# Weight maxima of two experts: from reloaded halves, or from the units as they pass

## The chip, the core and the metric

The kernel runs on one core of one Trainium2 chip. The metric is the device time of one execution in microseconds (us); the time given for a kernel is the median of its runs. A core has five engines that each work through their own queue in order: TensorE (PE, matrix products), VectorE (DVE), ScalarE (ACT), GpSimd (POOL) and SyncE (SP), which here issues nearly all DMA transfers.

## The reference, cut to what matters

Four batches of eight heads of causal attention with a decay, 576 positions of 64 columns, give x with 2304 rows of 512 columns. A mixture of four experts follows, with weights by domain and no routing: every row goes through every expert.

```python
scores = scale * q @ k.T + (cum[:, None] - cum[None, :])      # causal
x = softmax(scores) @ v                                       # 2304 x 512
p = domain_probs / domain_probs.sum(-1)
for e in range(4):
    h = relu(x @ w1[e])                                       # 512 -> 1024
    out += p[:, e:e+1] * (h @ w2[e])                          # 1024 -> 512
```

## The kernel before

**Two forms of a product.** Every product of float32 numbers is made from parts. In the first sweep over the weights a weight unit is split into a rounded part wh and a rest wl, both 128x1024 in a 32-bit matmul format. In the second sweep, and in everything behind it, the parts are float16, and a unit must first be scaled by a power of two that fits the largest weight of its expert. That is why the maximum of each expert's weights is needed, for w1 and w2 apart.

**Units and steps.** The weights of an expert lie in eight units of 128x1024 (512 KB): 512 columns of w1 and 512 of w2. Units 0 to 31 are the first sweep's, 32 to 63 the second's, with unit n holding the same numbers as n - 32. A step takes two units over a chunk of 256 rows of x: l1 (x times w1), a gate (gh on ACT, gl on DVE) and, while the next step's l1 is under way or done, l2. Two steps make a group of four units, and acc on DVE adds up each group. The name l1_0_6_2_1 means sweep 0, group 6 (expert 3 has groups 6 and 7), chunk 2, second half of the group. The first sweep has 28 steps (chunk 0 for every expert, 1 for experts 2 and 3, 2 for expert 3), at 60 to 250 us or so; steps 28 to 79 are the second sweep. Attention for the later chunks runs between: s is a score, p its exponential, z and pt its float16 parts before and behind a transposing DMA, o the product with v, and x of a chunk is made of four head pairs (0 to 3). y is x in float16; topx and ux find the scale of a chunk.

**Where maxima came from.** `w_peek(e, i)` loads half a unit (128x512, 256 KB) into the tile pk with a DMA on SP and, two steps on, reduces it on DVE to a column of wmax. For expert e it is called in 16 steps beginning at PEEK[e]: 1, 15, 31 and 45. In step PEEK[e] + 17 (18, 32, 48, 62) `w_scale(e)` follows: its first part reduces wmax to wm on DVE, writes wm to DRAM (dw) and reads it back spread over all partitions into tops; the second part, three steps later, makes the scale wsc and its inverse wun. `w_split(n)` takes a loaded unit wr: in the first sweep ACT rounds it to wh and DVE or POOL subtract to wl; in the second, it is scaled and split in float16, with assertions that its expert's scale is known. It then starts three later loads of units.

**What sets the order.** The program is written once, as a list of steps with attention's work spread by cost; a scheduler then gives each engine its queue from a model of the engines. A function under `behind` is kept behind the gl of the step before. `at_step(n, f)` runs f behind the gl in step n. An instruction added on one engine so moves others, on all engines.

Of the kernel before, what the change touches and what calls it, by code (L numbers as in the profile page):

```python
# [13 lines left out]
ALU = mybir.AluOpType  # L14
AX = mybir.AxisListType
# [12 lines left out]
    ((1, 2, 3, 4), (1, 2, 3, 4), (2, 3, 4), (3, 4)),  # L28
)
WIDE = (0, 1, 2)  # L30
PEEK = (1, 15, 31, 45)
V_PEEK = 1
PT = ("pth", "ptl", "ptx")
TURN = ((1, 14), (2, 18), (3, 24), (4, 28))
# [44 lines left out]
def fused(ctx: ExitStack, tc: tile.TileContext, qk, v, f, probs, w, out):  # L79
    nc = tc.nc  # L80
# [35 lines left out]
    wmax = const.tile([128, 2, 8, E], F32, name="wmax")  # L116
# [73 lines left out]
    def at_step(n, f):  # L190
        later.setdefault(n, []).append(f)
# [47 lines left out]
    def behind(f):  # L239
        if prev is None:  # L240
            f()
            return
        with tc.issue_after(prev.last.ins):
            f()
# [32 lines left out]
    def w_peek(e, i):  # L277

        n, k = divmod(i, 2)
        t = pk_p.tile([128, 512], F32, tag="pk", name=f"pk{e}_{i}")  # L280
        nc.sync.dma_start(out=t, in_=w[8 * e + n, :, 512 * k : 512 * k + 512])
        at_step(
            step + 2,
            lambda: nc.vector.tensor_reduce(
                out=wmax[:, k, n, e : e + 1], in_=t, op=ALU.max, axis=AX.X, apply_absolute_value=True
            ),
        )
# [57 lines left out]
    def v_peek(i):  # L345

        t = xf_p.tile([128, 1024], F32, tag=f"xf{2 + i % 2}", name=f"vp{i}")
        flat = v.rearrange("b r p t h d -> (b r p t h d)").rearrange(
            "(n p f) -> n p f", n=NV, p=128
        )  # L350
        nc.sync.dma_start(out=t, in_=flat[i])

        def top():
            with tc.issue_after(prev.first.ins):
                nc.scalar.activation(
                    out=t,
                    in_=t,
                    func=AF.Abs,
                    scale=1 / 1024,
                    accum_out=vmax[:, i : i + 1],  # L360
                )

        at_step(step + 2, top)
# [570 lines left out]
    def w_load(n):  # L934
        if n < NS and n not in wraw:
            wraw[n] = wr_p.tile([128, 1024], F32, tag="wr", name=f"wr{n}")
            nc.sync.dma_start(out=wraw[n], in_=w[n % 32])
# [3 lines left out]
    def w_pair(name):  # L941
        t = w_p.tile([128, 2, 1024], F16, tag=("wh", "wl")[len(pairs) % 2], name=name)
        pairs.append(t)
        return t

    def w_split(n):
        w_load(n)
        r = wraw.pop(n)
        if n < 32:
            wh[n] = w_p.tile([128, 1024], F32R, tag="wh", name=f"wh{n}")  # L950
            wl[n] = w_p.tile([128, 1024], F32R, tag="wl", name=f"wl{n}")
            nc.scalar.activation(out=wh[n], in_=r, func=AF.Copy)  # L952
            eng = nc.vector if n in W_DVE else nc.gpsimd
            for a in (0, 512):
                z = a + 512
                eng.tensor_tensor(  # L956
                    out=wl[n][:, a:z],
                    in0=r[:, a:z],
                    in1=wh[n][:, a:z].bitcast(F32),
                    op=ALU.subtract,  # L960
                )
        else:
            e = n % 32 // 8
            assert ("w", e) in known
            t = w_pair(f"w{n}")
            wh[n], wl[n] = t[:, 0], t[:, 1]
            for k in range(2):
                c = slice(512 * k, 512 * k + 512)
                sc = wsc[:, e, k : k + 1]
                if k == 1:  # L970
                    nc.gpsimd.tensor_scalar(  # L971
                        out=r[:, c], in0=r[:, c], scalar1=sc, scalar2=None, op0=ALU.mult
                    )
                    nc.scalar.activation(out=wh[n][:, c], in_=r[:, c], func=AF.Copy)
                    nc.gpsimd.tensor_tensor(
                        out=wl[n][:, c], in0=r[:, c], in1=wh[n][:, c], op=ALU.subtract
                    )
                    continue
                nc.scalar.activation(out=wh[n][:, c], in_=r[:, c], func=AF.Copy, scale=sc)
                nc.vector.scalar_tensor_tensor(  # L980
                    out=wl[n][:, c],
                    in0=r[:, c],
                    scalar=sc,
                    in1=wh[n][:, c],
                    op0=ALU.mult,
                    op1=ALU.subtract,
                )
            at_step(step + 2, lambda: nc.sync.dma_start(out=wd[n - 32], in_=t))
        w_load(n + 1)
        w_load(n + 2)  # L990
        w_load(n + 3)
# [629 lines left out]
    for n in range(len(steps) + 1):  # L1621
        step = n
        cur = steps[n] if n < len(steps) else None
        for f_ in later.pop(n, ()):
            behind(f_)
        for e, first_ in enumerate(PEEK):
            if 0 <= n - first_ < 16:
                w_peek(e, n - first_)
            if n == first_ + 17:
                a_, b_ = w_scale(e)  # L1630
                behind(a_)
                at_step(n + 3, b_)
        if 0 <= n - V_PEEK < NV:
            v_peek(n - V_PEEK)
        if n == V_PEEK + NV + 1:
            a_, b_ = v_scale()
            behind(a_)
            at_step(n + 2, b_)
        if cur is not None:
            if cur.c not in used:  # L1640
                used.add(cur.c)
                upto(need[cur.c])
            for c, m in TURN:
                if n >= m and c not in yh and ("x", c) in known:
                    narrow(c)
            if cur.s == 1:
                assert cur.c in yh
                weigh(cur.g // 2, cur.c)
            for q in range(4):
                cur.l1(q)  # L1650
                pace(n + q / 8)
            cur.gate()
        else:
            upto(len(asteps))
            chunks.close()
            late.h = late.enter_context(tc.tile_pool(name="h", bufs=4, side="right"))
            for e in range(E):
                weigh(e, LAST[0])
            big = [Big(p) for p in range(16)]
            turns = in_turns(0)  # L1660
            for _ in range(3):
                next(turns)()
        if prev is not None:
            for q in range(4):
                prev.l2(q)
                pace(n + (q + 4) / 8)
                if cur is None:
                    for _ in range(2 if q == 3 else 1):
                        next(turns)()
            for w0, t in ends.items():  # L1670
                if t is prev:
                    if w0 + 7 < NS:
                        w_split(w0 + 6)
                        w_split(w0 + 7)
                    first_units(w0)
        prev = cur
# [90 lines left out]
```

## Time and profile before

| | |
|---|---|
| median of 3 runs | 939.88 us (939.54 to 941.59) |
| the profiled execution | 939.25 us |
| span, first to last instruction | 937.5 us |
| PE, DVE, ACT, POOL busy | 885.3, 709.3, 568.9, 525.1 us |
| mean granted clock of TensorE | 0.985 |
| moved by DMA | 159.45 MB |

The span is 1.75 us shorter than the execution. A busy engine of 25 in a stretch of 25 us has no gap; a clock below 1.00 means that part of the stretch ran at the lower of two levels. An idle time in the timeline stands with the instruction that ended it, and with the engine, or the DMA, that came last.

### The profile page before, as it was taken

Reading aid. Unit: us, or ns where it says so; the run is one execution under the profiler, and the core shown is the slowest. Engines: PE = TensorE matmul, PEld = TensorE weight load, DVE = VectorE, ACT = ScalarE, POOL = GpSimd, SP = SyncE. Lnnn points to the kernel's source line nnn. Section 1 sums busy time; section 2 is a strip of 40 time slices with the busy share of each in tenths; the row PEclk is TensorE's granted clock in tenths of the full one; section 3 lists DMA queues with packets and bytes.
Section 4 is the critical chain, followed back from the end, with each engine's and each line's share of the span. In section 5 each row is a group of like instructions: output and inputs, shape, how many; then the busy total and the mean of one; then the engine's idle time right before and its main releaser. Section 6 shows DMA issues by size and latency. Waiting matters only on the chain. (4 is left out here: it accounts for less than half of the span.)

```text
span 937.5 us, 16657 instructions
## 1 busy us (share of the span) xinstructions
PE 885.3 (94%) x5783; PEld 620.8 (66%) x5783; DVE 709.3 (76%) x1458; ACT 568.9 (61%) x1137; POOL 525.1 (56%) x528
## 2 busy tenths in 40 slices
PE   4899998999998889999999989999998999999998
PEld 3699988999765556666666656654455664666547
DVE  5768665786888988789878887576778757786487
ACT  5869755465676778668666777355665345653350
POOL 4657865478533754327641684265778627785060
PEclk9999999999998988999999999999999999999999
DMA  7458844538879698988999699524322424232003
GB/s 264 146 176 295 291 126 164 186 119 313 227 189 198 152 293 195 311 156 212 306 288 158 119 328 236 135 67 142 129 91 81 145 68 125 79 107 74 23 1 91
DMA packets 147508, 159.45 MB, mean 170 GB/s; under 512 B 86148, under 2 KB 107328, under 8 KB 147424
## 3 DMA queue, kind: packets, MB, share of 16 engines
q1 hardware_dynamic: 147424, 158.39, 60.2%
q8 instruction: 45, 0.74, 0.3%
q14 instruction: 39, 0.32, 0.2%
HBM read 117.30 MB, written 21.65 MB: 148 GB/s over the span
## 5 line engine op out<-in xcount | busy, mean ns | idle before, releaser
L1012 PE MATMUL l<-y,w 128*128 128x256 f16 x1248 | 155.7, 275 | 0.0
L1012 PEld LDWEIGHTS <-w 128*128 128x128 f16 x1248 | 118.3, 99 | 30.6 <-issue 6.5
L644 ACT ACTIVATE p<-p,nm 128x576 f32<-128x576 f32 (+3 forms) x160 | 95.6, 598 | 52.4 <-DVE nm L629 43.5
L1045 PE MATMUL l<-w,gh 128*128 128x512 f16 x408 | 122.6, 383 | 4.8 <-DVE acc L1072 4.8
L714 DVE SCALAR_TENSOR_TENSOR z<-p,rs,z 128x384 f16<-128x384 f32 (+3 forms) x128 | 85.7, 694 | 12.6 <-ACT z L713 11.1
L1072 DVE SCALAR_TENSOR_TENSOR acc<-y,scg,acc 128x256 f32<-128x256 f32 (+1 forms) x164 | 81.1, 515 | 14.9 <-PE y L1283 14.7
L615 PE MATMUL s<-hi 128*128 128x384 f32 (+1 forms) x192 | 76.9, 406 | 16.1 <-DVE hi L577 8.9
L563 POOL CAST q<-raw 64x320 fp32r<-64x320 f32 (+1 forms) x56 | 26.0, 465 | 117.9 <-PE s L615 71.3
L1283 PE MATMUL m<-rh,bs 128*128 128x512 f16 x256 | 86.4, 379 | 0.0
L629 DVE CUSTOM_DVE_ANT_0 p<-s,mask 128x288 f32<-128x288 f32 (+2 forms) x160 | 74.8, 475 | 12.9 <-PE s L615 11.8
L571 POOL TENSOR_TENSOR kl<-raw,hi 64x576 fp32r<-64x576 f32 (+1 forms) x56 | 66.4, 1186 | 28.6 <-ACT hi L562 28.2
L1045 PE MATMUL l<-w,gl 128*128 128x512 f16 x204 | 77.1, 383 | 5.0 <-DVE gl L1026 5.0
L1209 POOL TENSOR_TENSOR bs<-wt,bs 128x512 f16<-128x512 f32 x32 | 38.4, 1201 | 75.7 <-ACT bs L1208 75.4
L971 POOL TENSOR_SCALAR wr<-wr,wsc 128x512 f32<-128x512 f32 x32 | 53.9, 1687 | 35.1 <-DMA wr<-in_w 25.5
L956 POOL TENSOR_TENSOR wl<-wr,wh 128x512 fp32r<-128x512 f32 x48 | 64.4, 1370 | 15.9 <-ACT wh L952 11.6
L713 ACT ACTIVATE z<-p,rs 128x384 f16<-128x384 f32 (+3 forms) x128 | 69.5, 589 | 4.6 <-issue 1.2
L1026 DVE SCALAR_TENSOR_TENSOR gl<-l,gh 128x512 f16<-128x512 f32 (+1 forms) x80 | 54.7, 684 | 19.1 <-ACT gh L1025 18.6
L1012 PE MATMUL l<-xh,wh 128*128 128x256 f32 x224 | 65.0, 292 | 0.8 <-ACT xh L857 0.8
L615 PE MATMUL s<-kl,q 66*128 66x384 f32 (+1 forms) x192 | 63.7, 336 | 2.2 <-DMA kl<-nc 2.2
L1283 PE MATMUL m<-rh,bw 128*128 128x512 f16 x191 | 64.4, 379 | 1.4 <-ACT r L1329 1.4
L1012 PE MATMUL l<-xl,wh 128*128 128x256 f32 x224 | 65.2, 291 | 0.0
L1045 PEld LDWEIGHTS <-gh 128*128 128x128 f16 x408 | 37.0, 98 | 42.2 <-issue 11.2
(387 smaller groups left out, 2359.6 us busy)
## 6 DMA issues: line engine op xcount, KB each, us to landing
wr<-in_w SPq DMA_DIRECT2D x90, 512.0 KB
pk<-in_w SPq DMA_DIRECT2D x64, 256.0 KB
wd<-w SPq DMA_DIRECT2D x32, 512.0 KB
raw<-in_qk SPq DMA_DIRECT2D x32, 448.0 KB
bw<-wd SPq DMA_DIRECT2D x32, 256.0 KB
bv<-wd SPq DMA_DIRECT2D x32, 256.0 KB
raw<-in_qk SPq DMA_DIRECT2D x24, 256.0 KB
vp<-in_v SPq DMA_DIRECT2D x10, 512.0 KB
```

What stands on the lines that cost most here:

```text
L571: eng.tensor_tensor(out=kl[:64, :wk], in0=r[:64, ko : ko + wk], in1=hi[:64, ko : ko + wk].bitcast(F32), op=ALU.subtract,)
L615: nc.tensor.matmul(out=ps[:, at : at + z - a], lhsT=lhsT, rhs=rhs, start=(m == 0), stop=(m == 1),)
L629: nc.vector.tensor_tensor_reduce(out=pt[:, a:z], in0=ps, in1=mask[:, m0 + a : m0 + z], scale=-0.125, scalar=BIG if n == 0 else nm[:, col : ...
L644: nc.scalar.activation(out=pt[:, :w_], in_=pt[:, :w_], func=AF.Exp, scale=-1.0, bias=self.nmax[hh][:, c : c + 1], accum_out=self.ssum[:, h ...
L713: nc.scalar.activation(out=o[:, 0], in_=x, func=AF.Copy, scale=sc)
L714: nc.vector.scalar_tensor_tensor(out=o[:, 1], in0=x, scalar=sc, in1=o[:, 0], op0=ALU.mult, op1=ALU.subtract)
L956: eng.tensor_tensor(out=wl[n][:, a:z], in0=r[:, a:z], in1=wh[n][:, a:z].bitcast(F32), op=ALU.subtract,)
L1012: nc.tensor.matmul(out=self.l1p[:, fi, :], lhsT=lhsT, rhs=rhs[:, k, :], start=(k == 0 and m == 0), stop=(k == 3 and m == 2),)
L1026: self.last = nc.vector.scalar_tensor_tensor(out=self.gl, in0=self.l1p, scalar=0.0, in1=self.gh.bitcast(F32) if wide else self.gh, op0=ALU ...
L1045: matmul(out=l2[tt], lhsT=lhsT, rhs=rhs, start=(self.ps == 0 and fi == 0 and m == 0), stop=(self.ps == 1 and fi == 1 and m == 2),)
L1072: nc.vector.scalar_tensor_tensor(out=acc[c][:, tt, d0:d1], in0=ps, scalar=sc, in1=acc[c][:, tt, d0:d1], op0=ALU.mult, op1=ALU.add,)
L1283: line.append(nc.tensor.matmul(**args))
```

## The change

`PEEK` keeps experts 0 and 1. For units 16 to 31, those of experts 2 and 3 in the first sweep, `w_split` takes the maximum of the raw unit: a reduce over both halves at once (128x2x512 to 128x2) on DVE, between the rounding on ACT and the subtraction. That takes the place of 32 loads and 32 reduces. `SCALE` sets the steps of `w_scale` apart from `PEEK`: 18 and 32 as they were, 37 and 42 in place of 48 and 62.

```diff
-PEEK = (1, 15, 31, 45)
+PEEK = (1, 15)
+SCALE = (18, 32, 37, 42)
...
             nc.scalar.activation(out=wh[n], in_=r, func=AF.Copy)
+            if n // 8 >= len(PEEK):
+                nc.vector.tensor_reduce(
+                    out=wmax[:, :, n % 8, n // 8],
+                    in_=r.rearrange("p (k c) -> p k c", k=2),
+                    op=ALU.max,
+                    axis=AX.X,
+                    apply_absolute_value=True,
+                )
             eng = nc.vector if n in W_DVE else nc.gpsimd
...
-            if n == first_ + 17:
-                a_, b_ = w_scale(e)
-                behind(a_)
-                at_step(n + 3, b_)
+        if n in SCALE:
+            a_, b_ = w_scale(SCALE.index(n))
+            behind(a_)
+            at_step(n + 3, b_)
```

**Chunk 2 at step 20, PE before.** o2_3_0_1 is the last head product of chunk 2 and b2_3_0 spreads its divisors; l1_0_6_2_0 begins with xh2, whose fourth slice is made from them (the rows for wh24 stand in groups of three per slice).

```order
L792 MATMUL o2_3_0_1_2222<-pth2_3_0_1_2159,v22_3_0_1830 128x128
L792 MATMUL o2_3_0_1_2222<-ptl2_3_0_1_2160,v22_3_0_1830 128x128
L682 MATMUL b2_3_0_2229<-ident_114,rb2_3_0_2122 128x128 x2
L1045 MATMUL l2_0_6_0_0_1_2575<-wh27_2382,gl0_6_0_1_2540 128x512
L1012 MATMUL l1_0_6_1_1_2699<-xh1_827,wh26_2375 128x256
...
L1012 MATMUL l1_0_6_1_1_2699<-xh1_827,wl27_2383 128x256
L1045 MATMUL l2_0_6_1_0_0_2762<-wh24_2052,gh0_6_1_0_2665 128x512
...
L1045 MATMUL l2_0_6_1_0_1_2777<-wh25_2059,gl0_6_1_0_2666 128x512
L1012 MATMUL l1_0_6_2_0_2792<-xh2_1621,wh24_2052 128x256
...
L1012 MATMUL l1_0_6_2_0_2792<-xh2_1621,wh24_2052 128x256
...
L1012 MATMUL l1_0_6_2_0_2792<-xh2_1621,wh24_2052 128x256
...
L1012 MATMUL l1_0_6_2_0_2792<-xh2_1621,wh24_2052 128x256
```

**The same, PE now.** The head product is among the rows of l1_0_6_2_1.

```order
L1021 MATMUL l1_0_6_2_1_2900<-xh2_1625,wh26_2385 128x256
L793 MATMUL o2_3_0_1_2232<-pth2_3_0_1_2169,v22_3_0_1836 128x256
L683 MATMUL b2_3_0_2239<-ident_114,rb2_3_0_2132 128x128 x2
L1021 MATMUL l1_0_6_2_1_2900<-xl2_1626,wh26_2385 128x256
...
L793 MATMUL o2_3_0_1_2232<-ptl2_3_0_1_2170,v22_3_0_1836 128x256
L793 MATMUL o2_3_0_1_2232<-pth2_3_0_1_2169,v22_3_0_1836 128x128
L793 MATMUL o2_3_0_1_2232<-ptl2_3_0_1_2170,v22_3_0_1836 128x128
L1021 MATMUL l1_0_6_2_0_2806<-xh2_1625,wh24_2060 128x256
L1021 MATMUL l1_0_6_2_1_2900<-xh2_1625,wh26_2385 128x256
L1021 MATMUL l1_0_6_2_0_2806<-xl2_1626,wh24_2060 128x256
```

The last row of o2_3_0_1 stood 48 rows ahead of the use of the fourth slice; now that use (the row of wh24) comes next behind it.

**Steps 30 to 32, PE before.** topx3 are the two small products that find chunk 3's scale; l1_1_0_3_0 is the first that reads y3, chunk 3 in float16.

```order
L199 MATMUL topx3_175<-ident_114,xmax_127 1x128
L615 MATMUL s0_0_1_1_2_0_3152<-hi0_0_1_1_2926 128x384
L615 MATMUL s0_0_1_1_2_0_3152<-kl0_0_1_1_2835,q2_1_117 128x384
...
L1012 MATMUL l1_1_0_2_1_3855<-y2_2600,w34_3546 128x256
L220 MATMUL topx3_175<-ux3_176,ones_r_131 128x1
...
L1012 MATMUL l1_1_0_2_1_3855<-y2_2600,w34_3546 128x256
...
L1045 MATMUL l2_1_0_2_0_1_3901<-w33_3092,gl1_0_2_0_3792 128x512
L615 MATMUL s0_1_1_1_4_0_3496<-hi0_1_1_1_3245 128x288
L615 MATMUL s0_1_1_1_4_0_3496<-kl0_1_1_1_3136,q2_1_117 128x288
...
L1012 MATMUL l1_1_0_3_0_3918<-y3_3185,w32_3084 128x256
```

**The same, PE now.** The s are attention's scores.

```order
L1054 MATMUL l2_1_0_2_0_1_3915<-w35_3570,gl1_0_2_1_3900 128x512
L200 MATMUL topx3_175<-ident_114,xmax_127 1x128
L616 MATMUL s0_0_1_1_2_0_3168<-hi0_0_1_1_2940 128x384
L616 MATMUL s0_0_1_1_2_0_3168<-kl0_0_1_1_2849,q2_1_117 128x384
...
L616 MATMUL s0_1_1_0_4_0_3341<-kl0_1_1_0_2945,q2_0_116 128x288
L221 MATMUL topx3_175<-ux3_176,ones_r_131 128x1
L616 MATMUL s0_1_1_0_4_1_3344<-hi0_1_1_0_3147 128x288
...
L616 MATMUL s0_1_1_1_3_0_3424<-kl0_1_1_1_3152,q2_1_117 128x512
...
L817 MATMUL o0_0_1_3456<-pt0_0_1_0_3073,v20_0_1_2937 64x320
L616 MATMUL s0_1_1_1_4_0_3512<-hi0_1_1_1_3261 128x288
L616 MATMUL s0_1_1_1_4_0_3512<-kl0_1_1_1_3152,q2_1_117 128x288
...
L1021 MATMUL l1_1_0_3_0_3930<-y3_3201,w32_3100 128x256
```

Between the first topx3 and the first use of y3 there stood l1 of chunk 2 and l2 of chunks 1 and 2, steps 29 to 31; now all of these are ahead of the first topx3, and what is left behind it is scores and the first row of o0_0_1.

**Transposes of pt0_3_1, SP before.** The rows run from the transposes of the first head to those of the second; kl, raw and vr are loads for later heads.

```order
L723 DMA_TRANSPOSE pt0_3_1_0_3942<-z0_3053 128x6x128
L723 DMA_TRANSPOSE pt0_3_1_0_3942<-z0_3053 128x8x128
L723 DMA_TRANSPOSE pt0_3_1_0_3942<-z2_3055 128x9x64
L516 DMA vr1_1_1_4151<-in_v 128x640
L537 DMA kl1_1_1_1_4269<-ncd_133 2x576
L512 DMA raw1_1_1_1_4271<-in_qk 128x896
L281 DMA pk2_6_4390<-in_w 128x512
L937 DMA wr43_4635<-in_w 128x1024
L723 DMA_TRANSPOSE pt0_3_1_1_4121<-z1_3054 128x6x128
L723 DMA_TRANSPOSE pt0_3_1_1_4121<-z1_3054 128x8x128
L723 DMA_TRANSPOSE pt0_3_1_1_4121<-z3_3056 128x9x64
```

**The same, SP now.** dw2 and its tops are the maxima of expert 2, written and read back.

```order
L724 DMA_TRANSPOSE pt0_3_1_0_3954<-z0_3069 128x6x128
L724 DMA_TRANSPOSE pt0_3_1_0_3954<-z0_3069 128x8x128
L724 DMA_TRANSPOSE pt0_3_1_0_3954<-z2_3071 128x9x64
L517 DMA vr1_1_1_4157<-in_v 128x640
L317 DMA dw2_4390<-wm2_4389 128x2
L538 DMA kl1_1_1_1_4272<-ncd_133 2x576
L513 DMA raw1_1_1_1_4274<-in_qk 128x896
L318 DMA tops_130<-dw2_4390 128x256
L724 DMA_TRANSPOSE pt0_3_1_1_4127<-z1_3070 128x6x128
L724 DMA_TRANSPOSE pt0_3_1_1_4127<-z1_3070 128x8x128
L724 DMA_TRANSPOSE pt0_3_1_1_4127<-z3_3072 128x9x64
```

The loads of pk2_6 and of the unit wr43 are gone from before the second head's transposes, and dw2 with its tops stands there.

## Rows read from the trace of the kernel before

**Rows 1.** The page's part 1: busy time, share of the span and instructions of each engine.

```profile
PE 885.3 (94%) x5783; PEld 620.8 (66%) x5783; DVE 709.3 (76%) x1458; ACT 568.9 (61%) x1137; POOL 525.1 (56%) x528
```

**Rows 2.** Table of stretches: us, busy time of each engine, PEclk, DMA share, GB/s.

```profile
125.00:150.00 25.00, 20.97 (x132) 18.89 (x131) 14.77 (x37) 12.80 (x28) 16.19 (x15) 0.93 0.51 147
150.00:250.00 100.00, 100.00 (x689) 91.08 (x688) 74.19 (x179) 59.53 (x134) 66.19 (x70) 1.00 0.58 190
250.00:275.00 25.00, 23.57 (x150) 15.53 (x148) 20.96 (x58) 15.47 (x31) 9.23 (x11) 1.00 0.98 238
275.00:300.00 25.00, 21.02 (x154) 14.49 (x153) 20.93 (x48) 18.44 (x41) 7.81 (x8) 0.86 0.89 182
300.00:325.00 25.00, 22.43 (x152) 14.14 (x150) 24.52 (x54) 20.28 (x41) 18.52 (x18) 0.93 0.65 157
325.00:350.00 25.00, 22.03 (x142) 14.58 (x139) 22.81 (x60) 15.78 (x34) 13.23 (x11) 0.90 1.05 286
350.00:375.00 25.00, 23.12 (x157) 16.18 (x158) 21.27 (x42) 19.77 (x39) 11.82 (x13) 0.83 0.89 200
375.00:525.00 150.00, 146.82 (x1089) 100.29 (x1087) 124.00 (x283) 102.20 (x206) 66.94 (x64) 1.00 0.97 234
```

**Rows 3.** Timeline of PE: start, length, instruction, [idle before <-releaser].

```profile
138.80 0.40 PE L1045 MATMUL l<-wh,gh 128*128 128x512 f32 x1
139.03 0.40 PE L1045 MATMUL l<-wl,gh 128*128 128x512 f32 x1
143.46 0.49 PE L792 MATMUL o<-pth,v 128*128 128x256 f32 x1 [4.03 <-ACT pth L752]
...
288.89 0.44 PE L816 MATMUL o<-pt,v 128*64 128x320 f16 x1 [3.98 <-DMA pt<-z]
...
345.98 0.69 PE L615 MATMUL s<-hi 128*128 128x384 f32 x1 [2.48 <-POOL hi L577]
```

**Rows 4.** Groups of instructions in 250 to 525 us: busy, mean ns | idle before.

```profile
L644 ACT ACTIVATE p<-p,nm 128x576 f32<-128x576 f32 (+2 forms) x78 | 54.5, 700 | 40.9 <-DVE nm L629 33.0 <-DVE ss L672 3.0 <-DVE wm L315 1.8
...
L562 ACT ACTIVATE hi<-raw 128x896 fp32r<-128x896 f32 x26 | 24.5, 944 | 9.1 <-issue 3.5 <-PE s L615 3.5 <-DMA raw<-in_qk 1.9
L284 DVE TENSOR_REDUCE wmax<-pk 128x1 f32<-128x512 f32 x36 | 24.1, 674 | 4.6 <-DMA pk<-in_w 4.6
...
L644 ACT ACTIVATION_READ_ACCUMULATOR p<-p,nm 128x1 f32 x77 | 14.4, 187 | 0.0
```

**Rows 5.** Timeline of ACT, then DVE, where x of chunk 2 is made.

```profile
178.84 0.38 ACT L827 ACTIVATE tmp<-o 64x256 f32<-64x256 f32 x1 [2.37 <-PE o L792]
...
181.47 0.42 ACT L857 ACTIVATE xh<-xs 128x256 fp32r<-128x256 f32 x1 [1.81 <-DVE xs L856]
...
179.32 0.75 DVE L1072 SCALAR_TENSOR_TENSOR acc<-l,prob,acc 128x512 f32<-128x512 f32 x1 [0.86 <-PE l L1045]
180.10 0.43 DVE L835 TENSOR_TENSOR xs<-o,tmp 64x256 f32<-64x256 f32 x1
...
182.26 1.21 DVE L260 TENSOR_REDUCE xmax<-xh 128x1 f32<-128x1024 f32 x1
```

**Rows 6.** Waits, of 250 to 400 us, then SP's: us, times, longest.

```profile
POOL wr L971 <- DMA wr<-in_w: 16.7, 5, 4.3
...
SPq L317 <- DMA dw<-wm: 12.1, 4, 3.6
```

**Rows 7.** Timeline of PE, ACT and DVE in steps 29 to 32.

```profile
250.15 0.42 PE L615 MATMUL s<-hi 128*128 128x384 f32 x1
...
251.34 0.39 PE L1045 MATMUL l<-w,gh 128*128 128x512 f16 x1
...
268.69 1.05 PE L1012 MATMUL l<-y,w 128*128 128x256 f16 x8
...
265.86 1.15 ACT L475 ACTIVATE y<-xf,xsc 128x1024 f16<-128x1024 f32 x1
...
267.04 1.29 DVE L476 SCALAR_TENSOR_TENSOR y<-xf,xsc,y 128x1024 f16<-128x1024 f32 x1 [0.79 <-ACT y L475]
```


## Prediction

> **What bounds the kernel now.** I read the page first for who is busy: TensorE (PE) works for 94% of the span [rows 1]. So the end is set by PE's work, its stalls and its clock. The change leaves PE the same instructions; only their order, the stalls and the clock can move the time. Next I read the table of 25 us stretches for where PE loses time [rows 2]. From 150 to 250 us it loses nothing: busy 100 of 100 at clock 1.00. The losses lie in 125 to 150 (4.0 us idle, clock 0.93) and in 250 to 375: 1.4, 4.0, 2.6, 3.0 and 1.9 us idle, 12.9 together, with the clock at 0.83 to 0.93 in the last four. Lost clock is worth as much: the full clock is 2.4 GHz and the lower level 1.2, and a mean of 0.86 over 25 us is 3.5 us of full-speed time gone; for the four stretches 3.5 + 1.75 + 2.5 + 4.25 = 12.0 us. Then I read PE's timeline for who ends each stall [rows 3]. At 284.91 PE waits 3.98 us for a probability tile pt, whose transposes stood on the sync queue (SP) behind the load of tops from dw1. Until 345.98 it waits 2.48 us for hi, a GpSimd (POOL) product; POOL stood five times between 250 and 400 us, 16.7 us in all, for a weight tile wr that had not landed [rows 6], and in 325 to 350 the DMA engines read 1.05 busy. In 300 to 325 VectorE (DVE) is busy 24.5 of 25 us. The removed work lies there and behind it: of the 36 reduces of pk in 250 to 525 us [rows 4], 32 are those of experts 2 and 3.
>
> **Removed and added work.** Removed are 32 loads of 256 KB (128x512 of four bytes) and 32 reduces at 0.674 us [rows 4], 21.6 us of DVE. Added are 16 reduces of 128x2x512. The nearest row is a reduce over 1024 elements per partition, 1.21 us [rows 5], so 16 x 1.21 = 19.4 us, or 21.6 at twice the half size. DVE's total is the same within 2 us. The Trainium skill's page "VectorE: DVE Perf Modes", section "The perf-mode tier table", says that tensor_reduce has only a 1x form, so reducing more at once saves nothing but the start; the rows bear this out (1.21 against 2 x 0.674), and by its rule alone the sum here would be 21.6 instead of 19.4 us, a saving of nothing.
>
> The load is only moved: into steps 6 to 21, 97 to 200 us, where PE never waits now except at 139. There DVE goes from 74 of 100 us [rows 2] to some 90. Cover by idle DVE time looks ample, so I don't charge the reduces as such. What I charge is the order. The maxima of a unit are queued on DVE ahead of the gates and of attention's work, and the scheduler, which sees DVE later, puts attention later against the MoE steps on PE, up to 7 us of PE work at step 31. Step 37 and 42 instead of 48 and 62 for w_scale move dw2, dw3 and their two loads of tops ahead on SP.
>
> **Places where the new order exposes a wait.**
> - Chunk 1, step 10. Between the last matmul of o1_3_0_1 and the first use of pair 3 of x there are now ten matmuls of 512 columns and nine of 256. At 0.23 us from start to start [rows 3], and half of that for 256, that is 3.3 us of cover. The chain needs tmp, xs, v, acc, the maximum of unit 23 (1.21) and xl on DVE: the second acc (0.75) [rows 5] follows the last of the ten matmuls, 2.3 us on, so with 0.42 for xl, as long as xh, 2.3 + 0.75 + 1.21 + 0.42 = 4.7 us. The use of xl is one matmul later than that of xh, at 3.4, so 1.2 to 1.3 us are open, up to 3 if unit 23 lands late. I take 1.5.
> - Chunk 2, step 20. Before, 13 matmuls of 512 columns and 33 of 256, 6.8 us, stood between the end of o2_3_0_1 and the use of pair 3 of x2; now there are none. The chain is tmp 0.38, xs 0.43, v, the product with b, xh 0.42 and xl, the three others about as long as xs [rows 5], 2.5 us. PE stalls 2.5 (1.5 to 3.5); with the clock 1.5 more (0 to 2).
> - Units 25 and 26: DVE meets their reduces ahead of the gate gl0_5_0_1, and both tiles come late, behind SP's wait for dv, whose stall of 4.03 us until 143.46 [rows 3] stays as it is. 1.0 (0 to 1.5).
> - Chunk 3, step 31 to 32. Before, topx3 and the first matmul on y3 are 18.5 us apart, filled with the work of steps 29 to 31 [rows 7]. Now only attention scores stand there. After the gate PE has 24 matmuls of 512 columns (5.5 us) and ten score pairs; three of them, one of each width, take from 250.15 to 251.34 [rows 7], 0.40 each, so 4.0 us, together 9.5. ScalarE (ACT) must do six exponentials at 0.70 + 0.19, two hi at 0.94 [rows 4] and y3 1.15, and DVE y3 1.29 [rows 7]. The first exponential can begin some 6.5 us after the gate (5.5, a pair, and a minimum on DVE at 0.6, an estimate between DVE's 0.43 for 256 and 0.75 for 512 columns [rows 5]), so y3 is ready at 6.5 + 5.3 + 1.9 + 1.15 + 1.29 = 16.1. The stall would be 6.6; I take 6.0 (3 to 7), since the first matmul may need only ACT's half of y3. The next matmul group, o0_0_1, follows and waits for its transposes another 1.5 (0 to 2.3). Clock: a stall of 4 us came with 1.75 us of lost clock at 125 to 150 and with 3.5 at 275 to 300 [rows 2]; I take 3.0 for this one (1.75 to 4.25).
> Sum of what is new: 1.5 + 2.5 + 1.5 + 1.0 + 6.0 + 1.5 + 3.0 = 17.0 us.
>
> **Places where a wait goes.** In 250 to 300 the order in which o0_0_1 stands makes the stalls of 1.4 and 4.0 us go, and of the 3.5 us of clock 2.5: 7.9. In 300 to 375 the POOL queue now has the hi of the next head ahead of the late weight tile, and DVE loses 0.674 us for each pk reduce; but acc waits now behind gl and wm2, and the clock there depends on all stalls at once. Of 7.4 us idle and 8.5 of clock I take back 3.5; nothing at one end, 16 at the other. From 375 to 525 PE is idle 3.2 us in all [rows 2], and the DMA engines stay busy with the other loads; 1.5 (0 to 3.2).
> What is late next after the pk loads are gone from SP: dw2 and its tops now stand there, just before the transposes of pt0_3_1_1, and dw3 before those of pt1_2_1_0. SP stands 12.1 us in 4 such waits, the longest 3.6 [rows 6]. I cost them at nothing, because the pk loads and weight loads that stood there before took as long; without that cover each costs up to 4 us. The Trainium skill's "DMA: Bandwidth & Descriptors", section "Anatomy of one DMA", puts a small transfer at about 2 us fixed, mostly the receipt of the write; the measured mean of 3.0 us is longer, and by the page's figure the two blocks would come to about 4 us instead of 6.
>
> **Sum.** 17.0 - 7.9 - 3.5 - 1.5 = +4.1 us on the profiled execution's 939.25 us, 943.4. The median of the runs is 0.63 us above that execution, so 944.0 us.
>
> **The rivals.**
> - Relief where it was wanted (faster). One mechanism: the stalls of 300 to 375 hang on DVE and on weight loads that queue behind pk loads; without these they vanish, and with them half of the clock lost there (7.4 + 4.6). It takes back 12 us instead of 3.5: 944.0 - 8.5 = 935.5. For it: DVE 24.5 of 25 in 300 to 325, DMA 1.05, and pk loads queued on SP ahead of weight tiles. Against: half of the idle time there is the POOL queue's order. The sign turns where 7.6 us are taken back, and 9.5 make it faster by 0.2%. Chance 0.25.
> - The order costs less than it looks (no change): PE's queue at step 31 still stands, but chunk 1, 2 and the clock don't add, so that the sum ends within a microsecond of before, 940. For it: DVE is idle for 26 of the 100 us from 150 to 250. Chance 0.20.
> - The change doesn't shorten what it claims: SP's new waits for dw2 and dw3 each hold the transposes that stand behind them, as dw1's did at 284.91, 3.98 us each, and the chunk chains stall as charged: 944.0 + 8 = 952. For it: the row of 284.91. Against: the transposes are needed later in the new order. Chance 0.15.
> My forecast has 0.40.
>
> **How the numbers follow.** About 0.2%, 1.9 us, is what a measurement of this kernel can tell from no change; so faster is below 938.0 and slower above 941.8. The forecast's own range is 941 to 948 by its unknown ends. Faster: 0.25 from the first rival, 0.02 from the forecast's lower end, 0.27. Same: 0.18 of the second rival's 0.20 and 0.03 of the forecast, 0.21. Slower: the forecast's other 0.35, the third's 0.15 and 0.02 of the second's, 0.52. The range for 8 in 10 takes in the first rival's centre and the start of the last: 934 to 952.
>
> **What would show it.** Right: PE busy below 25 in 175 to 200 with a stall ended by xh or xs of chunk 2; a stall of 5 us or more ended by y3 between 255 and 275; no stall on pt at 285; no stall on hi at 343. Wrong: 150 to 250 still at 25.00 and the y3 chain covered; or the stretches 300 to 375 at clock 1.00, which is the first rival; or two waits of 4 us on pt behind tops, which is the third. A time below 938 would mean that relief outweighed order.

## The result, and the profile after

The changed kernel takes 951.50 us (median of 4 runs, 949.27 to 954.77) against 939.71 for the kernel before (4 runs, 937.55 to 941.59); the ratio is 1.0122, 95% interval 1.0093 to 1.0152. It is slower, as forecast, and by three times as much: 11.8 us where 4.1 were forecast. The profiled execution is the slowest of the four, 954.77 us with a span of 953.0, so its own difference to the profile of before is 15.5 us.

The page's first part has PE 8.5 us busier than in [rows 1], for the same 5783 matmuls:

```profile
PE 893.8 (94%) x5783; PEld 625.8 (66%) x5783; DVE 718.5 (75%) x1442; ACT 571.2 (60%) x1137; POOL 522.0 (55%) x528
```

PE's idle time rose from 52.2 us (937.5 - 885.3) to 59.2. So 7 us of the 15.5 are waits, and for 8.5 us more PE is busy with the same products, at a mean granted clock of 0.966 instead of 0.985. (At 25 to 50 us this execution's clock read 0.59, but PE was busy there for 20.3 us against 20.9 before, so that little of the 8.5 us lies there.)

To compare stretches in which the work is shifted, I take four regions: 75 to 250 us (first sweep), 250 to 325 (chunk 3 becomes y3), 325 to 425, and 425 to 650 (rest of the second sweep). In each, what PE loses is its idle time, the length less PE busy, and the clock, (1 - PEclk) times the length. Columns: stretch, length, busy time of PE, PEld, DVE, ACT, POOL, then PEclk, DMA share, GB/s. The kernel before:

```profile
75.00:250.00 175.00, 170.97 (x1158) 155.84 (x1157) 125.95 (x303) 111.01 (x245) 120.07 (x127) 0.99 0.64 209
250.00:325.00 75.00, 67.02 (x451) 44.16 (x449) 66.41 (x158) 54.19 (x111) 35.56 (x36) 0.93 0.84 192
325.00:425.00 100.00, 94.61 (x678) 64.89 (x676) 84.29 (x191) 67.56 (x136) 39.46 (x38) 0.93 0.96 240
425.00:650.00 225.00, 217.79 (x1520) 141.37 (x1518) 175.03 (x358) 144.34 (x285) 120.19 (x111) 1.00 0.79 203
```

The changed kernel:

```profile
75.00:250.00 175.00, 165.00 (x1083) 150.58 (x1082) 132.64 (x293) 100.47 (x222) 108.49 (x118) 0.97 0.63 193
250.00:325.00 75.00, 70.82 (x478) 49.52 (x476) 67.80 (x164) 55.60 (x116) 35.39 (x38) 0.93 0.78 190
325.00:425.00 100.00, 86.58 (x572) 56.12 (x571) 80.57 (x175) 68.72 (x138) 57.51 (x55) 0.90 0.83 207
425.00:650.00 225.00, 222.31 (x1613) 149.37 (x1612) 170.80 (x352) 147.46 (x292) 105.48 (x97) 1.00 0.74 182
```

Lost by this reckoning: before 5.8, 13.2, 12.4, 7.2 us, together 38.6; after 15.3, 9.4, 23.4, 2.7, together 50.8. The first sweep loses 9.5 more and 325 to 425 loses 11.0 more; the other two give back 8.3. The remaining 3 us of the profile's difference lie outside these regions or in the rounding of the clock, worth up to 1 us in the longest region. Each region is one execution's, and the runs of the kernel before alone lie between 934.73 and 944.96 us, so a difference of 2 or 3 us in one region says little.

**What the reduces do on DVE.** The group of the new reduces in the changed kernel (busy, mean ns | idle before, releaser):

```profile
L955 DVE TENSOR_REDUCE wmax<-wr 128x2 f32<-128x1024 f32 x16 | 19.4, 1215 | 10.8 <-DMA wr<-in_w 10.8
```

Each takes 1.215 us, as the prediction had it; and DVE stands 10.8 us in front of them for units that have not landed. PE's stalls that follow, from its timeline:

```profile
122.26 0.58 PE L1021 MATMUL l<-xl,wh 128*128 128x256 f32 x1 [4.24 <-DVE xl L859]
...
198.68 0.50 PE L1021 MATMUL l<-xh,wh 128*128 128x256 f32 x2 [2.28 <-ACT xh L858]
...
345.55 0.74 PE L817 MATMUL o<-pt,v 128*64 128x320 f16 x4 [3.31 <-DMA pt<-z]
...
408.75 0.59 PE L1054 MATMUL l<-w,gh 128*128 128x512 f16 x1 [3.10 <-DVE acc L1081]
```

At 118 us the stall ends with xl of chunk 1. DVE's timeline there shows why it is 4.24 us:

```profile
116.77 0.75 DVE L1081 SCALAR_TENSOR_TENSOR acc<-l,prob,acc 128x512 f32<-128x512 f32 x1
120.65 1.22 DVE L955 TENSOR_REDUCE wmax<-wr 128x2 f32<-128x1024 f32 x1 [3.13 <-DMA wr<-in_w]
121.79 0.41 DVE L859 TENSOR_TENSOR xl<-xs,xh 128x256 fp32r<-128x256 f32 x1
```

The second acc is done at 117.5, DVE then waits 3.13 us for unit 23, reduces it, and only then makes xl. At chunk 2 the stall is the bare chain, 2.28 us.

**What stands on the sync queue.** From SP's timeline, where the maxima of expert 2 go out and come back:

```profile
334.53 0.33 SPq L317 DMA_DIRECT2D dw<-wm  x1
...
339.20 0.32 SPq L318 DMA_DIRECT2D tops<-dw  x1
339.61 3.89 SPq L724 DMA_TRANSPOSE pt<-z  x3
```

From 335.6 to 339.2 the queue stands, and the transposes of pt0_3_1_1 and the loads of units 43 and 44 behind it start late; PE's stall of 3.31 us is that of the transposes. Waits in 325 to 425 us; the first of them came to 13.1 us in four waits in the same stretch of the kernel before (the 16.7 of [rows 6] are those of 250 to 400 us):

```profile
POOL wr L980 <- DMA wr<-in_w: 25.5, 7, 9.1
...
PE o L817 <- DMA pt<-z: 4.0, 2, 3.3
```

### The profile page after: what moved, and what is told of

It reads as the page before. It is cut to its first block, busy times and chain, and to the rows that moved or that the text cites. A ratio compares the mean times of both kernels' runs of the same rounds, so it can differ in the third digit from the quotient of the medians.

```text
span 953.0 us, 16607 instructions
## 1 busy us (share of the span) xinstructions
PE 893.8 (94%) x5783; PEld 625.8 (66%) x5783; DVE 718.5 (75%) x1442; ACT 571.2 (60%) x1137; POOL 522.0 (55%) x528
## 4 chain that ended last, share of the span: by engine, by line
PE 32%; POOL 11%; DVE 10%; ACT 6%; DMA 5%; issue 5%; SPq 0%; POOLq 0%; DVEq 0%; ACTq 0%
PE y L1292 8%; PE m L1292 7%; PE l L1054 7%; PE l L1021 7%; POOL s L1352 4%; DMA wr<-in_w 3%; POOL wt L1186 3%; DVE z L715 2%; PE s L616 2%; PE o L817 2%; DVE p L630 1%; POOL wu L1186 1%; DMA pt<-z 1%; DVE acc L1081 1%; DVE rl L1173 1%
## 5 line engine op out<-in xcount | busy, mean ns | idle before, releaser
L715 DVE SCALAR_TENSOR_TENSOR z<-p,rs,z 128x384 f16<-128x384 f32 (+3 forms) x128 | 88.7, 720 | 9.5 <-ACT z L714 8.1
L1081 DVE SCALAR_TENSOR_TENSOR acc<-y,scg,acc 128x256 f32<-128x256 f32 (+1 forms) x164 | 81.1, 515 | 14.9 <-PE y L1292 14.7
L1021 PE MATMUL l<-xl,wh 128*128 128x256 f32 x224 | 67.6, 302 | 4.2 <-DVE xl L859 4.2
L1034 ACT ACTIVATE gh<-l 128x512 f16<-128x512 f32 (+1 forms) x80 | 47.0, 588 | 37.0 <-PE l L1021 36.5
L1021 PE MATMUL l<-xh,wl 128*128 128x256 f32 x224 | 66.9, 299 | 0.1
```

Of the source, the lines that this page charges most:

```text
L715: nc.vector.scalar_tensor_tensor(out=o[:, 1], in0=x, scalar=sc, in1=o[:, 0], op0=ALU.mult, op1=ALU.subtract)
L1021: nc.tensor.matmul(out=self.l1p[:, fi, :], lhsT=lhsT, rhs=rhs[:, k, :], start=(k == 0 and m == 0), stop=(k == 3 and m == 2),)
L1081: nc.vector.scalar_tensor_tensor(out=acc[c][:, tt, d0:d1], in0=ps, scalar=sc, in1=acc[c][:, tt, d0:d1], op0=ALU.mult, op1=ALU.add,)
```

## The experiments

The change has three parts that can be set apart: A, the new reduces of raw units in the first sweep; B, the scales at 37 and 42 instead of 48 and 62; C, the 32 loads and reduces of pk left out. The table has every run with its ratio to the kernel before (measured beside it) and what PE loses in the four regions of its profile, reckoned as above, from one execution each.

| kernel | parts | median us | ratio (95%) | 75-250 | 250-325 | 325-425 | 425-650 |
|---|---|---|---|---|---|---|---|
| before | - | 939.7 | 1 | 5.8 | 13.2 | 12.4 | 7.2 |
| e3_reduces_added | A | 950.99 | 1.0134 (1.0083-1.0185) | 11.5 | 8.2 | 14.9 | 12.0 |
| e6_early_scale_loads_kept | A B | 955.43 | 1.0172 (1.0153-1.0191) | 12.3 | 8.5 | 30.2 | 3.5 |
| e1_late_scale | A C | 952.53 | 1.0149 (1.0117-1.0181) | 11.4 | 9.2 | 15.1 | 11.1 |
| the change | A B C | 951.50 | 1.0122 (1.0093-1.0152) | 15.3 | 9.4 | 23.4 | 2.7 |
| e4_loads_removed | C | 942.05 | 1.0028 (1.0007-1.0049) | 5.7 | 6.2 | 16.4 | 11.5 |
| e7_early_scale_no_maxima | B C | 940.26 | 1.0010 (0.9993-1.0026) | 3.5 | 7.5 | 21.5 | 2.5 |
| e2_defer_reduce | A later, B C | 948.94 | 1.0127 (1.0088-1.0165) | 12.6 | 8.4 | 20.7 | 2.7 |
| e5_defer_late | A later, C | 944.90 | 1.0060 (1.0040-1.0079) | 8.6 | 9.4 | 13.3 | 10.8 |
| e9_expert3_only | half of A, half of C | 943.43 | 1.0047 (1.0029-1.0065) | 10.1 | 6.2 | 14.3 | 9.2 |
| e12_expert2_only | half of A, half of C | 940.81 | 1.0008 (0.9989-1.0026) | 8.5 | 6.5 | 12.1 | 10.0 |
| e10_expert3_deferred_early | half of A later, half of C, B for 3 | 941.77 | 1.0024 (1.0010-1.0039) | 5.7 | 4.5 | 20.0 | 8.9 |
| e11_tiny_reduces | A without its time, C | 940.07 | 0.9999 (0.9976-1.0022) | 2.2 | 9.3 | 9.6 | 12.3 |
| e13_dve_relieved | A C, DVE relieved | 930.75 | 0.9889 (0.9858-0.9920) | 8.7 | 5.0 | 0.4 | 12.6 |

### Scales late again

```diff
-SCALE = (18, 32, 37, 42)
+SCALE = (18, 32, 48, 62)
```

> The change with w_scale of experts 2 and 3 back at steps 48 and 62; loads of pk stay out, maxima still come from the units. Theory S (the sync queue): the 12 us that the changed kernel loses between steps 36 and 46 come from dw2 and dw3, whose waits of 4 us now stand ahead of transposes and weight loads of units 43 to 50. Then this kernel gets most of them back: 940 to 943 us, with the gates of step 46 at about 12 us behind before instead of 24. Theory O (the order of PE in the first sweep and at chunk 3, by the DVE work added): nothing comes back, 949 to 952.

952.53 us, no faster than the change and just above what theory O gave. Its regions:

```profile
75.00:250.00 175.00, 167.10 (x1111) 152.46 (x1110) 137.01 (x298) 103.53 (x228) 113.15 (x121) 0.98 0.63 196
250.00:325.00 75.00, 71.02 (x474) 48.32 (x473) 67.85 (x162) 56.24 (x117) 35.85 (x39) 0.93 0.76 186
325.00:425.00 100.00, 89.86 (x635) 62.16 (x636) 81.07 (x183) 70.22 (x142) 44.81 (x42) 0.95 0.86 202
425.00:650.00 225.00, 216.20 (x1541) 142.80 (x1539) 170.66 (x345) 142.31 (x281) 116.08 (x108) 0.99 0.76 190
```

In 325 to 425 us it loses 15.1 instead of 23.4, so the early maxima did cost 8.3 there, as theory S said; but in 425 to 650 it loses 11.1 instead of 2.7. What the early scales cost at 335 and 383 comes back behind 425 us, where the late ones stand; which wait it is there was not traced. Theory S had the place and not the balance.

### The reduces alone, added to the kernel before

```diff
             nc.scalar.activation(out=wh[n], in_=r, func=AF.Copy)
+            if n // 8 >= 2:
+                nc.vector.tensor_reduce(out=wmax[:, :, n % 8, n // 8], in_=r..., op=ALU.max, ...)
```

> The kernel before, with the 16 new reduces of the raw units added and nothing taken away (the maxima of experts 2 and 3 are found twice). If the cost sits in the reduces of the first sweep (waits for weight loads on DVE, the order), this is 6 to 10 us slower than before, 946 to 950, with 5 us lost at chunk 1. If it sits in the sync queue's early dw2 and dw3, this is within 3 us of before apart from the 4 us of chunk 1: 941 to 944.

950.99 us, 11.2 more than before: the whole loss of the change, with nothing taken away and the scales where they were. Chunk 1's stall is 2.96 us and chunk 2's 2.28; the 5 us at chunk 1 that I expected were too many.

### The loads of pk removed, nothing put in

```diff
-PEEK = (1, 15, 31, 45)
+PEEK = (1, 15)
+SCALE = (18, 32, 48, 62)
...
+        nc.gpsimd.memset(wmax[:, :, :, 2:], 0.1)
...
```

> The kernel before, with the 32 loads of pk of experts 2 and 3 and their reduces removed and nothing put in their place: the maxima of experts 2 and 3 are a constant 0.1, so no maximum of theirs is taken; w_scale stays at 48 and 62. It measures what the removal alone is worth. First rival of the prediction (relief in 263 to 505 us): 928 to 934. My forecast's 5 us of relief in 300 to 525: 933 to 936. If the DMA and DVE share there never bounded PE: 939 to 941.

942.05 us: 8.4 MB of DMA and 21.6 us of DVE less, and no gain; if anything 0.3% is lost. This refutes the first rival of the prediction and my own 5 us of relief. Its regions:

```profile
75.00:250.00 175.00, 171.10 (x1159) 156.07 (x1158) 126.77 (x305) 111.76 (x247) 121.37 (x128) 0.99 0.62 208
250.00:325.00 75.00, 68.83 (x491) 46.78 (x488) 69.11 (x160) 55.07 (x114) 36.66 (x36) 1.00 0.81 185
325.00:425.00 100.00, 90.62 (x652) 62.48 (x650) 73.11 (x174) 66.67 (x135) 38.37 (x38) 0.93 0.83 196
425.00:650.00 225.00, 217.96 (x1509) 141.38 (x1508) 168.20 (x340) 144.36 (x283) 118.23 (x109) 0.98 0.72 189
```

The loss moved. PE's longest wait in it, and POOL's rows behind it:

```profile
347.44 0.69 PE L617 MATMUL s<-hi 128*128 128x384 f32 x1 [6.64 <-POOL hi L579]
...
343.11 1.59 POOL L973 TENSOR_SCALAR wr<-wr,wsc 128x512 f32<-128x512 f32 x1 [6.11 <-DMA wd<-w]
344.65 0.44 POOL L565 CAST q<-raw 64x320 fp32r<-64x320 f32 x1
345.07 1.39 POOL L573 TENSOR_TENSOR kl<-raw,hi 64x576 fp32r<-64x576 f32 x1
346.54 0.85 POOL L579 TENSOR_TENSOR hi<-raw,hi 64x320 fp32r<-64x320 f32 x1
```

PE waits 6.64 us for a hi of POOL; POOL had stood 6.11 us in front of the scaling of weight unit 46 before it came to that head's kl and hi. (The unit's load was issued at 337.93 on SP; the releaser that the row names is another transfer.) In the kernel before, POOL's queue had the scaling of unit 46 behind hi1_1_1_1; with the loads and their reduces gone, the schedule has all of units 43 to 46 ahead of hi1_1_1_1 and hi1_2_1_0. PE's wait for that hi, 2.48 us in [rows 3], became one of 6.64. Both kernels that keep the loads and the late scales (before, e3) have unit 46 behind hi1_1_1_1; e1 and e5, which do without the loads, have it ahead, and stalls of 7.40 and 6.57 us at that place. No run has the loads out and this queue as before, so what their removal is worth without the new order is not shown.

### Maxima from the rounded copy, two steps later

```diff
-                nc.vector.tensor_reduce(out=wmax[...], in_=r..., ...)
+                at_step(step + 2, lambda h=wh[n]: nc.vector.tensor_reduce(
+                    out=wmax[...], in_=h.bitcast(F32)..., ...))
```

> The change, with each unit's maximum taken from wh, the rounded copy, two steps later behind the gate, so that DVE never stands for a weight load. Theory S and the chunk-1 chain: the stall of 4.24 us at 118 us, that of 2.41 at 145 and the lost clock behind them go, the rest stays: 944 to 947. Theory O (the amount of DVE work put early moves the order of PE): 949 to 952, and chunks 2 and 3 still stall.

948.94 us (ratio 1.0127, its runs 945.56 to 951.89). The stall at 118 us is gone, that at 137 is 5.07 us, chunk 2's 2.28 is as it was. The median lies between the two expectations; the ratio's interval, which beside 939.8 us is 948 to 955, takes in theory O's and not theory S's. With runs that scatter so far I don't decide by this one alone.

> Maxima from the rounded copy two steps later, and w_scale of experts 2 and 3 back at 48 and 62. Theory D (what costs is the DVE work of the maxima put into the first sweep; where dw2 and dw3 stand is neutral, since what they cost early they give back late): the same as with the early scales, 948 to 950. Theory S (the early dw2 and dw3 cost on top, hidden in the earlier run by chance): 942 to 945.

944.90 us, 7.6 less than with the raw units and late scales, where theory D (the amount of DVE work is what counts) expected no difference. In this kernel DVE does the same work and stands for no unit:

```profile
L957 DVE TENSOR_REDUCE wmax<-wh 128x2 f32<-128x1024 f32 x16 | 18.7, 1210 | 0.0
```

So with late scales most of the cost of A goes when the reduces no longer wait for a landing; 2.9 us are left against e4_loads_removed. PE's order is not what went: chunk 2's stall of 2.28 us, ended by xh, stands in this kernel too. The time lies in the range that I gave for theory S, but not by its reason, since late scales gained nothing with the raw units. That deferring is worth 7.6 here, but with early scales 2.6 by the medians and nothing by the ratios (1.0127 against 1.0122), is not explained.

### The other corners of the table

> The change with the 32 loads of pk and their reduces of experts 2 and 3 put back (the maxima are found twice): new reduces and early w_scale, nothing removed. Theory D: like the new reduces alone, 949 to 952. If the removal of the loads pays for something as soon as the scales are early, this is slower than the change, 954 to 958, by the 5 us that the change gets back after 425 us.

955.43 us, dearer than A alone by 4.4 and than the change by 3.9; in 325 to 425 it loses 30.2. So the removed loads are worth some 4 us where the scales are early, and nothing where they are late (e3 against e1, before against e4). Theory D was wrong here, the other expectation right.

> Loads and reduces of pk of experts 2 and 3 removed, no reduces put in (their maxima are a constant 0.1, none is taken), w_scale at 37 and 42: the change without its new reduces. Theory D: no more than 2 us from the kernel with the loads removed alone, 939 to 943. Theory S: 945 to 950. If relief in 300 to 525 us comes only with early scales: 932 to 937.

940.26 us. Without the new reduces the change would be no slower than before, and no faster. Its regions in the table have the same trade as the change, 21.5 in 325 to 425 and 2.5 behind.

A is thus worth 11.2 (before to e3), 10.5 (e4 to e1) and 11.2 us (e7 to the change), the same in the three settings that have both runs; early scales with the loads kept (e6) were not run without A. The place of the loss is not the same: with the loads out (e4 to e1) PE loses 8.7 us more up to 325 us and less behind it, with the loads kept (before to e3) 0.7 more up to 325 and 7.3 behind it. So A as the cause is shown, and one path for all of its loss is not.

### Half of the maxima

Experts 2 and 3 apart: the condition on n // 8 takes one of them, the other keeps its loads of pk.

> Only expert 3's maxima from the units (8 reduces, units 24 to 31, steps 14 to 21), expert 2 from pk loads as before, scales at 48 and 62. Theory D in proportion to the reduces: half of the 11 us, 944 to 947. By places: chunk 1's stall of 2.4 to 4.2 us at 118 us needs units 16 to 23 and is gone, chunk 2's head product now ends 40 rows and more ahead of its use, so nothing is lost up to 250 us and the time is 940 to 943.

> Only expert 2's maxima from the units (8 reduces, units 16 to 23, steps 6 to 12), expert 3 from pk loads at 45 as before, scales at 48 and 62: the other half of the run with expert 3 alone. If the two halves add up to the whole (952.5, with 942 for the loads removed and nothing put in), this is 949 to 952, and most of the loss is chunk 1's. If what costs needs both halves (DVE behind by more than the slack up to chunk 3), it is 943 to 946, as the other half.

943.43 and 940.81 us, against 942.05 with C alone: +1.4 and -1.2, where both together are +10.5. (Each half keeps 16 of the 32 loads, and no run has half of C alone; against the kernel before the halves are 0.5% and 0.1% slower.) The halves don't add up. The second lies below both of its ranges, and the first loses 10.1 up to 250 us, 4.4 more than C alone, where I expected nothing to be lost. My expectation that chunk 1 holds most of the loss fell too: expert 2's half has chunk 1's stall in full (3.06 us) and loses 8.5 up to 250, 2.8 more than with C alone, but it gets that back in 325 to 425 (12.1 against 16.4). The loss needs both halves. So does chunk 2's stall on PE: the 2.28 us ended by xh stand in the profiles of the change, e1, e2, e3, e5 and e6, which have all 16 full reduces, and in neither half. That DVE must be behind through the whole first sweep fits this and was not tested by itself.

### A wait without the work, and the work without the extra load

The first: each new reduce takes 8 columns of either half instead of 512.

```diff
-                    in_=r.rearrange("p (k c) -> p k c", k=2),
+                    in_=r.rearrange("p (k c) -> p k c", k=2)[:, :, :8],
```

> The change with late scales (48, 62), and each of the 16 new reduces over 8 columns of either half instead of 512: the other columns are left out of the maximum. DVE still stands in its queue for each unit to land, but for 0.1 us of work instead of 1.2, and PE's order is that of before at chunks 1, 2 and 3. Theory W (what costs is DVE standing for units that have not landed): 949 to 952, with the stalls at 118 and 141 us. Theory T (what costs is the 19 us of DVE time and the order of PE that follows from it): 940 to 943, as with the loads removed and nothing put in.

940.07 us. The group of its reduces:

```profile
L955 DVE TENSOR_REDUCE wmax<-wr 128x2 f32<-128x16 f32 x16 | 2.6, 164 | 11.0 <-DMA wr<-in_w 11.0
```

DVE stands as long for the units, 11.0 us, and nothing is lost; the stall at 118 us is gone. PE's order at chunks 1 to 3 is all but that of before, and chunk 2's stall is gone too. Theory W, the wait as such, is refuted: these waits cost something only together with the DVE time of full reduces, or with the order of PE that goes with it.

The second: all 16 full reduces, and the loads and reduces of pk of experts 0 and 1 out.

```diff
-PEEK = (1, 15)
-SCALE = (18, 32, 37, 42)
+PEEK = ()
+SCALE = (18, 32, 48, 62)
...
+        nc.gpsimd.memset(wmax[:, :, :, :2], 0.1)
...
-            if n // 8 >= len(PEEK):
+            if n // 8 >= 2:
```

> The changed kernel with late scales (48, 62) and all 16 full reduces of raw units, and with the loads and reduces of pk of experts 0 and 1 taken away (their maxima are a constant 0.1, none is taken): 32 reduces or 21.6 us of DVE less in steps 3 to 33, so DVE has about as much to do in the first sweep as in the kernel before, and PE's order at chunks 2 and 3 is again that of before. If the sum of DVE time in the first sweep decides (theory T): 939 to 943, though DVE still waits for units to land. If the place of these reduces decides (1.2 us each just ahead of the gates and of x): 948 to 952.

930.75 us, 21.8 less than e1_late_scale with the same new reduces, and 1.1% faster than before: below both ranges. DVE waits more than ever:

```profile
L956 DVE TENSOR_REDUCE wmax<-wr 128x2 f32<-128x1024 f32 x16 | 19.4, 1212 | 12.4 <-DMA wr<-in_w 12.4
```

but PE's order at chunks 2 and 3 is nearly that of before (no stall ended by xh at chunk 2), and 325 to 425 is almost without loss:

```profile
75.00:250.00 175.00, 169.80 (x1136) 154.23 (x1135) 130.16 (x289) 109.25 (x241) 117.39 (x123) 0.98 0.49 162
250.00:325.00 75.00, 70.04 (x513) 47.65 (x512) 71.55 (x166) 59.48 (x125) 37.99 (x37) 1.00 0.87 200
325.00:425.00 100.00, 99.62 (x731) 68.62 (x729) 85.81 (x194) 73.15 (x147) 51.86 (x49) 1.00 0.82 198
425.00:650.00 225.00, 216.93 (x1479) 138.00 (x1479) 165.02 (x323) 140.83 (x276) 115.02 (x110) 0.98 0.72 189
```

With as much less for DVE to do elsewhere in the sweep the loss is gone, though the reduces stand where they stood. That speaks for the sum of DVE's work and against the place of the reduces, but it doesn't rule the place out: no run has all loads of pk out and no reduces in, so what the 16 reduces cost in this setting is not shown. Nor is the sum enough by itself: e5 has the work of e1, and chunk 2's stall, and loses 2.9 us beside e4, not 10.5. With late scales the loss takes the work (e11) and the waits (e5) together. Why e13 is faster than before by 9.7 us isn't settled: by the table it is in 325 to 425 (12.4 lost before, 0.4 here; the rest about cancels), where POOL's queue now has hi1_1_1_1 ahead of units 44 and 45 and hi1_2_1_0 ahead of unit 46; but the run also moves 8.4 MB less before that, and I had no run that sets the two apart. It leaves out maxima and so is no version to use.

### A version put together

> A version put together from what the runs gave: expert 2 from pk loads with its scale at 48, expert 3 from the rounded copies of its units two steps later with its scale at 42. If the 4.7 us that early scales gave back after 425 us come from expert 3's (at 506 us before), and eight deferred reduces cost 1 to 2: 937 to 940, no slower than before and perhaps faster. If the early scale's blocks cost as much at 385 as they give back later: 942 to 945.

941.77 us, ratio 1.0024 (1.0010 to 1.0039), between the two ranges. With expert 3's scale early PE loses 20.0 us in 325 to 425, and 425 to 650 comes back only to 8.9. No version that takes all maxima beat the kernel before.

## Why the prediction was right in direction and short in size

- **Direction and cause.** It put the loss on the order that PE takes when DVE has more to do in the first sweep, and not on the reduces' own time. e3 (A alone is the whole loss), e11 (the same waits without the time cost nothing) and e13 (the same reduces, with DVE relieved, and no net loss) bear out that DVE's load in the first sweep is part of it. They don't separate DVE's time from the order of PE, since the schedule writes the second from the first, and no run has the reduces in and PE's order of before. e5 limits the reading: chunk 2's stall stays, and without the waits for landings 2.9 us are lost. How the loss divides between order and waits stays open.
- **First sweep: 6.5 us forecast, 9.5 measured.** Chunk 2 was 2.5 and is 2.28. Chunk 1 was 1.5, up to 3 if unit 23 landed late; DVE waited 3.13 us for it and the stall is 4.24. I had the mechanism, and even its upper end was too small. The clock was 1.5 and is 3.5 more than before. The 4.03 us at 143 that were to stay, with 1.0 more for units 25 and 26, are 2.41 instead, ended by p at 147.16.
- **Chunk 3, 250 to 300: +2.6 forecast (10.5 new, 7.9 gone), -1.1 measured.** The prediction's terms are for 250 to 300, 300 to 375 and 375 to 525 us, not for the four regions. The changed kernel in these three:

```profile
250.00:300.00 50.00, 47.20 (x300) 33.41 (x299) 43.91 (x104) 34.27 (x72) 22.34 (x24) 0.90 0.76 199
300.00:375.00 75.00, 64.78 (x438) 42.81 (x437) 67.25 (x157) 55.56 (x115) 41.88 (x42) 0.91 0.81 186
375.00:525.00 150.00, 144.00 (x1037) 97.04 (x1035) 115.93 (x255) 107.64 (x215) 78.12 (x69) 0.98 0.88 214
```

That is 7.8, 17.0 and 9.0 us lost, where [rows 2] give 8.9, 15.9 and 3.2. (The changed kernel runs behind by then, so each window ends a little earlier in its work.) The chain was right. ACT's gate of the last half before y3 starts at 271.70 and the matmul that needs all of y3 at 287.38:

```profile
271.70 0.60 ACT L1034 ACTIVATE gh<-l 128x512 f16<-128x512 f32 x1 [0.23 <-PE l L1021]
...
284.71 1.13 ACT L476 ACTIVATE y<-xf,xsc 128x1024 f16<-128x1024 f32 x1
...
287.38 1.01 PE L1021 MATMUL l<-y,w 128*128 128x256 f16 x4 [0.90 <-DVE y L477]
```

That is 15.7 us against a forecast of 16.1. What I mis-sized is what PE loses in it. I counted 6.0 of stall, 3.0 of clock and 1.5 for o0_0_1; PE was idle only 2.4 us in 275 to 300, and the clock took 5.0 (PEclk 0.80 there). The score pairs were spread thin over the chain, and the later ones ran at the lower level; the first row is the whole stretch:

```profile
275.00:300.00 25.00, 22.60 (x131) 15.27 (x129) 21.75 (x61) 18.72 (x40) 8.88 (x11) 0.80 0.60 109
275.00:277.50 2.50, 2.50 (x14) 1.23 (x12) 2.50 (x6) 0.00 (x0) 0.00 (x0) 1.00 0.61 150
277.50:280.00 2.50, 2.04 (x11) 1.42 (x10) 2.47 (x10) 1.12 (x3) 0.45 (x1) 1.00 0.03 0
280.00:282.50 2.50, 1.93 (x10) 1.14 (x8) 2.46 (x11) 2.50 (x8) 1.93 (x2) 0.90 0.38 41
282.50:285.00 2.50, 2.10 (x5) 1.27 (x5) 1.23 (x8) 2.50 (x6) 2.18 (x4) 0.50 0.47 98
285.00:287.50 2.50, 1.60 (x6) 1.01 (x6) 2.14 (x4) 2.48 (x4) 1.17 (x2) 0.50 0.40 125
287.50:290.00 2.50, 2.50 (x13) 1.72 (x12) 2.40 (x6) 2.45 (x6) 0.00 (x0) 0.50 1.16 216
```

- **300 to 375: -3.5 forecast, +1.1 measured; 375 to 525: -1.5 forecast, +5.8 measured.** This is the step that failed, "of 7.4 us idle and 8.5 of clock I take back 3.5", and the 1.5 behind it. Nothing came back. The third rival's mechanism came in its place: dw2 and dw3 hold SP, the loads of units 43 and 44 are issued behind dw2 at 343.6 us, POOL stands 25.5 us for units in 325 to 425 instead of 13.1, and PE's stalls and a lower clock follow. I had costed these blocks at nothing because loads stood there before. With the scales late, 325 to 425 loses 8.3 us less (e1). That is no fixed price: from e4 to e7 the same step costs 5.1 there and from e3 to e6 15.3, and why was not followed. The 2 us that the prediction cites from the Trainium skill's "Anatomy of one DMA" are given there for transfers that GpSimd issues; these are SP's, and the two waits took 6.1 us together.
- **Behind 425 us: a gain that the prediction did not have.** In 425 to 650, which overlaps the last window above, the change loses 4.5 us less than before, with e1 and e4 showing no gain there at all. All three pairs have it: with the scales no longer late, 8.4 (e1 to the change), 9.0 (e4 to e7) and 8.5 us (e3 to e6) less are lost there. What the early scales cost and what they give back nearly cancel: e1 and the change take the same time.
- **The signs.** The stall ended by xh of chunk 2 came, and the stalls on pt at 285 and on hi at 343 are gone. The stall of 5 us or more on y3 did not come, it is 0.90 us. Of two waits of 4 us on pt behind tops, the third rival's sign, one of 3.31 us came.
- **The rivals.** The first, relief by 12 us, fell with e4 and e7: the loads that went were not what PE waited for, or the wait changed its name (hi behind other units). (Half of the 8.5 us of clock in its sum is 4.3, not 4.6; nothing hangs on it.) The second, no change, is what B and C give without A, but its own mechanism, an order that costs little, did not hold. The third was right on the mechanism in 325 to 425, but its 8 us are given back later, and the loss that remains is A's: that its total, 952, is the measured one is luck. The forecast's own 941 to 948 was missed; the time lies at the upper end of the wide range, which that rival had set.

## What to carry to other kernels

A cheaper way to the same number is not cheaper if it moves work into a stretch that has no stall now: ask what the order of the bounding engine becomes there, and test the added part alone on top of the old kernel. Removing loads from a stretch with stalls need not be worth anything, even where DMA is busy, until the queue that stalls has been shown to wait for those loads; here the schedule put other units in their place. Two halves of a change that each cost little can cost much together, so test the whole and not the halves alone.

## What the runs showed of the hardware

A stall need not show as idle time. Between 277.5 and 282.5 us PE was busy 1.93 to 2.04 of each 2.5 us, with gaps of less than 1 us, and then worked at a granted clock of 0.50, the lower of its two levels (1.2 of 2.4 GHz), to 290 us: the 2.4 us of idle time in 275 to 300 came with 5.0 us of clock. A reduce over 16 columns took 164 ns, over 512 columns 674 ns and over 1024 columns 1215 ns, so joining two halves saves some 130 ns of 1350.
